# Mean square for the normalisation by two float32r products with a matrix of ones

## The chip, the cores and the metric

The kernel runs on one core of a Trainium2 chip. The metric is the device time of one execution in microseconds (us); the median over several runs is compared. All times below are in us unless ns is written. The engines are called as in the profile: PE is TensorE, PEld its loading of weights, DVE is VectorE, ACT is ScalarE, POOL is GpSimd, SP is SyncE.

## The reference

Attention with two kinds of masks is followed by a gated feed-forward layer with a normalisation by the root of the mean square (RMS) ahead of it. Everything is float32.

```python
# attention: batch 8, heads 8, 576 positions, 64 per head; a window of 32 (first heads)
# or of 32 steps of 4 (last heads)
attn = softmax(mask(q @ k.T / 8)); attn_out = attn @ v
x = attn_out.transpose(0, 2, 1, 3).reshape(4608, 512)
# feed-forward: 512 -> 1536 -> 512
rms = np.sqrt(np.mean(x * x, axis=-1, keepdims=True) + 1e-06)
xn = x / rms * rms_g
g = xn @ w_gate
val = xn @ w_val
return (g * (1.0 / (1.0 + np.exp(-g))) * val) @ w_out
```

## The kernel before

The 4608 tokens are cut into 16 units of 288 (U). x is held transposed: 128 of the 512 features on the partitions, tokens along the row, so a unit's x is four tiles of 128 x 288 (`xraw`). While the feed-forward products of one unit run on TensorE, the attention of the next is slipped in between. The first unit's products are plain float32; from the second unit on each float32 operand is split into a high part rounded to float32r and the remainder, also in float32r, and a product is three float32r products (`three`, lines 632 to 634).

**The plan.** Nothing is scheduled by the compiler: the program's order is written by hand. A unit's feed-forward is 36 steps (`now`): for each of 12 slices j of the hidden layer one step for the gate (g), one for the value (v) and one for the projection (acc) of the slice before. A dictionary `events` says in which step an attention piece has its scores (q, line 499, tile s), its transposition (t), its product with v (o), and in which step the unit's sum of squares (`rms_sum`) and its broadcast (`rms_apply`) stand. These TensorE instructions come at the end of the step, behind its twelve large products. Work on other engines is put off with `later(dt, rank, fn)`: it is issued dt steps on, at the step's start, in order of rank. EARLY and LAST set the steps of a unit's first and last scores, SCORES those of the second and third unit.

**The normalisation.** ScalarE squares each tile of x (line 433), VectorE or GpSimd adds the four up (line 439), which leaves 128 x 288 squares (`sq`). `rms_sum` sums over the partitions: three float32 products per unit, with 96 tokens of the squares as weights and a column `inv` of 1/512 as the moving operand, two columns wide, so that the mean of each token lands on a partition (96 x 3, tile rps). `rms_root`, one step later, adds 1e-6 on VectorE (line 546), takes the power -0.5 on GpSimd (line 547) and splits the result (rst_hi, rst_lo, lines 552 and 553). One step later `spread` multiplies the identity with each part, the high part on VectorE (line 561), the low one on ScalarE (line 565): tiles rd, 96 x 288 with the values on diagonals. `rms_apply` multiplies a matrix of ones with both (line 581, tile bps): every partition then has every token's factor, and VectorE applies it to x (line 595).

**Neighbours on the engines.** Around this stand, on VectorE, the gate's and value's products (lines 676 and 689, tile th), the masked maximum of scores (lines 366 and 371), the low part of q (line 349, tile qs) and the softmax's sum and reciprocal (lines 390 and 391); on GpSimd the low parts of the hidden layer (line 701, hlo), of k (line 340, ks) and the softmax's scaling (line 397).

## Time and profile before

| what | value |
|---|---|
| median of 3 runs | 1138.24 us (1136.36 to 1138.36) |
| the profiled execution's span, first to last instruction | 1137.1 us |
| what the median has beyond that span | 1.1 us |
| TensorE busy | 1119.5 us, 98% of the span |
| VectorE, ScalarE, GpSimd busy | 70%, 62%, 54% |
| the sums of squares (line 539): instructions, busy on TensorE | 96 in 16 units, 9.5 us |
| the broadcasts (line 581): instructions, busy on TensorE | 32, 7.4 us |
| mean granted TensorE clock | 0.997 |

One execution was profiled; its rows are read against its own span. A row of the view in order of time has start, length, engine, line, operation, tiles (written <- read), shape and, in brackets, how long the engine had been idle and what ended that. Records of TensorE overlap, since its products are pipelined: the distance from start to start is what one costs. A row of the view by groups has a count behind the x, then busy time, mean length of one in ns, and the idle time before them.

### The profile page before, as it was taken

What the parts mean: (1) busy time and instruction counts of PE and PEld (TensorE: products, weight loads), DVE (VectorE), ACT (ScalarE), POOL (GpSimd) and SP (SyncE); (2) the same over time, 40 slices, a digit from 0 to 9 for tenths busy, and PEclk for the clock granted to TensorE, in tenths of its full rate; (3) what the DMA queues carried; (4) which work ended last, traced back from release to release, by engine and by line L of the source; (5) the groups of instructions that cost most, each with busy time, mean ns of one, the idle gap of its engine ahead of it and who ended that gap; (6) DMA issues with size and microseconds to landing.
All of it is one profiled execution on the core that took longest, in us unless ns stands there. A gap on an engine that the chain in (4) does not pass through costs nothing.

```text
span 1137.1 us, 25931 instructions
## 1 busy us (share of the span) xinstructions
PE 1119.5 (98%) x8371; PEld 1088.7 (96%) x8371; DVE 795.5 (70%) x2875; ACT 708.7 (62%) x2608; POOL 615.7 (54%) x1071
## 2 busy tenths in 40 slices
PE   9999889999999999999999999999999999999998
PEld 7787779999999999999999999999999999999998
DVE  6889878858667585876758677675867768586411
ACT  6795665657667566675757666575766757576311
POOL 8223677656556455565646556564655646465311
PEclk9999989999999999999999999999999999999999
DMA  9665221212213031221213122121311212120000
GB/s 246 181 228 198 78 59 40 82 40 71 64 34 98 27 95 42 79 62 31 81 40 103 41 63 74 36 84 39 86 51 54 87 34 79 42 80 15 6 17 22
DMA packets 61545, 82.19 MB, mean 72 GB/s; under 512 B 7298, under 2 KB 41090, under 8 KB 61410
## 3 DMA queue, kind: packets, MB, share of 16 engines
q1 hardware_dynamic: 61410, 80.54, 23.7%
q8 instruction: 67, 1.10, 0.4%
q14 instruction: 68, 0.56, 0.2%
HBM read 71.08 MB, written 9.44 MB: 71 GB/s over the span
## 4 chain that ended last, share of the span: by engine, by line
PE 91%; DVE 5%; ACT 1%; issue 1%; DMA 1%; POOL 1%; POOLq 0%; SPq 0%; ACTq 0%
PE acc L632 9%; PE v L632 8%; PE g L632 8%; PE acc L633 8%; PE acc L634 8%; PE v L633 8%; PE g L633 8%; PE v L634 8%; PE g L634 8%; PE s L499 3%; PE o L487 3%; PE acc L629 2%; PE v L629 1%; PE o L488 1%; PE busy L749 1%; PE g L629 1%
## 5 line engine op out<-in xcount | busy, mean ns | idle before, releaser
L701 POOL TENSOR_TENSOR hlo<-th,hhi 128x288 fp32r<-128x288 f32 x180 | 146.3, 813 | 200.9 <-ACT hhi L700 150.6
L634 PE MATMUL acc<-hhi,lo 128*128 128x288 f32 x720 | 212.6, 295 | 0.0
L397 POOL TENSOR_SCALAR t<-t,sum 72x72 f32<-72x72 f32 (+3 forms) x414 | 153.1, 382 | 69.7 <-DVE sum L391 61.1
L634 PE MATMUL v<-xhi,lo 128*128 128x288 f32 x612 | 180.5, 295 | 0.0
L634 PE MATMUL g<-xhi,lo 128*128 128x288 f32 x612 | 180.3, 295 | 0.0
L700 ACT CAST hhi<-th 128x288 fp32r<-128x288 f32 x180 | 78.1, 434 | 155.7 <-DVE th L689 153.4
L381 ACT ACTIVATE t<-t,sum 96x128 f32<-96x128 f32 (+3 forms) x448 | 166.1, 375 | 11.4 <-DVE sum L371 10.9
L310 POOL TENSOR_TENSOR vlo<-vt,vhi 128x128 fp32r<-128x128 f32 x196 | 94.1, 480 | 107.6 <-ACT vhi L306 92.7
L671 ACT ACTIVATE th<-g 128x288 f32<-128x288 f32 x180 | 73.8, 410 | 106.1 <-PE g L634 86.3
L634 PEld LDWEIGHTS acc<-hhi,lo 128*128 128x128 f32 x720 | 135.9, 189 | 0.0
L427 DVE TENSOR_TENSOR xraw<-o,xraw 64x72 f32<-64x72 f32 (+1 forms) x364 | 99.1, 272 | 50.6 <-ACT xraw L417 44.5
L676 DVE SCALAR_TENSOR_TENSOR th<-th,g 128x288 f32<-128x288 f32 x180 | 80.4, 447 | 68.3 <-ACT th L671 68.3
L634 PEld LDWEIGHTS v<-xhi,lo 128*128 128x128 f32 x612 | 115.4, 189 | 0.0
L634 PEld LDWEIGHTS g<-xhi,lo 128*128 128x128 f32 x612 | 115.2, 188 | 0.0
L632 PE MATMUL g<-xhi,hi_g 128*128 128x288 f32 x357 | 111.0, 311 | 0.1
L632 PE MATMUL acc<-hhi,hi_o 128*128 128x288 f32 x360 | 111.0, 308 | 0.0
L366 DVE TENSOR_TENSOR t<-s,mask 96x256 f32<-96x256 f32 (+3 forms) x196 | 71.5, 365 | 53.5 <-PE s L499 42.6
L689 DVE TENSOR_TENSOR th<-th,v 128x288 f32<-128x288 f32 x180 | 81.4, 452 | 38.0 <-PE v L634 30.1
L633 PE MATMUL acc<-hlo,hi_o 128*128 128x288 f32 x360 | 107.3, 298 | 0.0
L340 POOL TENSOR_TENSOR ks<-qk,ks 128x288 fp32r<-128x288 f32 (+2 forms) x110 | 104.5, 964 | 0.3 <-ACT ks L335 0.3
L417 ACT COPY xraw<-o 64x72 f32<-64x72 f32 (+1 forms) x364 | 94.1, 259 | 11.7 <-PE o L488 9.6
L633 PE MATMUL g<-xlo,hi_g 128*128 128x288 f32 x322 | 94.9, 295 | 0.0
(192 smaller groups left out, 3597.0 us busy)
## 6 DMA issues: line engine op xcount, KB each, us to landing
qk<-in_qk_dram SPq DMA_DIRECT2D x60, 288.0 KB, 2.8
vt<-in_v_dram SPq DMA_DIRECT2D x196, 64.0 KB, 1.9
qk<-in_qk_dram SPq DMA_DIRECT2D x30, 352.0 KB, 3.0
out_dram<-ot SPq DMA_DIRECT2D x64, 144.0 KB, 1.9
qk<-in_qk_dram SPq DMA_DIRECT2D x30, 304.0 KB, 2.8
raw<-in_w_gate_dram SPq DMA_DIRECT2D x12, 512.0 KB, 4.6
raw<-in_w_val_dram SPq DMA_DIRECT2D x12, 512.0 KB, 4.9
raw<-in_w_out_dram SPq DMA_DIRECT2D x12, 512.0 KB, 4.2
```

Source lines behind the costliest of these rows:

```text
L310: G.tensor_tensor(out=vl, in0=vs.pop(b), in1=vh, op=ALU.subtract)
L340: ek.tensor_tensor(out=ks[:, 1, :nkt], in0=kr, in1=ks[:, 0, :nkt], op=ALU.subtract)
L381: A.activation(out=t[:nq, a, :n], in_=t[:nq, a, :n], func=AF.Exp, scale=-1.0, bias=sm[:nq, a, 0:1], accum_out=sm[:nq, a, 1:2] if u or i % ...
L397: (V if u == 0 and (c, i) > (NC - 1, 0) else G).tensor_scalar(out=t[:nq, a, :n], in0=t[:nq, a, :n], scalar1=sm[:nq, a, 3:4], scalar2=1.0, ...
L417: A.copy(out=to[a * D:(a + 1) * D], in_=o[a * D:(a + 1) * D, (2 + a) * nq:(3 + a) * nq])
L427: V.tensor_tensor(out=to[rows], in0=o[rows, a * nq:(a + 1) * nq], in1=to[rows], op=ALU.add)
L632: PE.matmul(out, wh[:, cc, :], xh, start=start, stop=False)
L633: PE.matmul(out, wh[:, cc, :], xl, start=False, stop=False)
L634: PE.matmul(out, wl[:, cc, :], xh, start=False, stop=stop)
L676: V.scalar_tensor_tensor(out=t, in0=t, scalar=1.0, in1=g, op0=ALU.add, op1=ALU.mult)
L689: V.tensor_tensor(out=t, in0=t, in1=v_ps[:, :U], op=ALU.mult)
L701: G.tensor_tensor(out=lo, in0=t, in1=hi, op=ALU.subtract)
```

## The change

From the second unit on, the sum over the partitions is taken by two float32r products in place of three float32 ones. The added-up squares are split into a high and a low float32r part (ScalarE casts, VectorE subtracts). Both are moving operands of 288 columns, and the weights are 96 columns of ones. Every one of the 96 partitions then holds all 288 sums. The wanted value of token q of block i on partition q is picked out on VectorE: a product with the identity (96 x 288), a sum along each block of 96, and the factor 1/512 with the 1e-6 added. The power, the splitting and the broadcast are as before. The plan moves too: EARLY and LAST are one less, so that the attention of each unit from the fourth on comes one step sooner; the sum stays 28 steps behind the unit's start and the broadcast 30 (from the third unit on), and in the second unit the sum comes one step later.

```diff
-EARLY, LAST = -9, 17
+EARLY, LAST = -10, 16
...
             later(1, 0.4, lambda: (V if c == NC - 1 or u == 1 else G).tensor_tensor(out=xsq[u], in0=xsq[u], in1=sq, op=ALU.add))
+            if u and c == NC - 1:
+                later(1, 0.45, lambda: square_parts(u))
...
+    def square_parts(u):
+        hi = sb.tile([P, U], F32R, tag="tmp", name=f"sqhi_{u}", bufs=2)
+        A.copy(out=hi, in_=xsq[u])
+        lo = sb.tile([P, U], F32R, tag="tmp", name=f"sqlo_{u}", bufs=2)
+        V.tensor_tensor(out=lo, in0=xsq[u], in1=hi, op=ALU.subtract)
+        xsq[u] = hi, lo
+
     def rms_sum(u):
-        r_ps = ps.tile([QB, NB, 2], F32, tag="o", name=f"rps_{u}")
-        for i in range(NB):
-            PE.matmul(r_ps[:, i, :], xsq[u][:, i * QB:(i + 1) * QB], inv, start=True, stop=True)
-        later(1, 0.1, lambda: rms_root(u, r_ps))
         if u == 0:
+            r_ps = ps.tile([QB, NB, 2], F32, tag="o", name=f"rps_{u}")
+            for i in range(NB):
+                PE.matmul(r_ps[:, i, :], xsq[u][:, i * QB:(i + 1) * QB], inv, start=True, stop=True)
+            later(1, 0.1, lambda: rms_root(u, r_ps))
             later(1, 6, spread_first)
+            return
+        r_ps = ps.tile([QB, U], F32, tag="o", name=f"rps_{u}")
+        for k, part in enumerate(xsq.pop(u)):
+            PE.matmul(r_ps, ones[:, :QB], part, start=k == 0, stop=k == 1)
+        later(1, 0.1, lambda: rms_root(u, r_ps.rearrange("p (i q) -> p i q", i=NB)))
 
     def rms_root(u, r_ps):
         r = sb.tile([QB, NB], F32, tag="rst", name=f"rst_{u}", bufs=2)
-        V.tensor_scalar(out=r, in0=r_ps[:, :, 0], scalar1=1e-6, scalar2=None, op0=ALU.add)
-        G.tensor_tensor(out=r, in0=r, in1=mhalf, op=ALU.pow)
         if u == 0:
+            V.tensor_scalar(out=r, in0=r_ps[:, :, 0], scalar1=1e-6, scalar2=None, op0=ALU.add)
+            G.tensor_tensor(out=r, in0=r, in1=mhalf, op=ALU.pow)
             rst[u] = [r]
             return
+        d = sb.tile([QB, NB, QB], F32, tag="tmp", name=f"diag_{u}", bufs=2)
+        V.tensor_tensor(out=d, in0=r_ps, in1=ident[:QB, None, :QB].to_broadcast([QB, NB, QB]), op=ALU.mult)
+        V.tensor_reduce(out=r, in_=d, axis=mybir.AxisListType.X, op=ALU.add)
+        V.tensor_scalar(out=r, in0=r, scalar1=1.0 / DM, scalar2=1e-6, op0=ALU.mult, op1=ALU.add)
+        G.tensor_tensor(out=r, in0=r, in1=mhalf, op=ALU.pow)
...
-        events.setdefault(last + (4 if u == 1 else 3), {})["sum"] = u
-        events.setdefault(last + (4, 7, 5)[min(u, 2)], {})["apply"] = u
+        events.setdefault(last + (3, 5, 4)[min(u, 2)], {})["sum"] = u
+        events.setdefault(last + (4, 7, 6)[min(u, 2)], {})["apply"] = u
```

What that makes of the order on the engines is shown for one unit in the middle of the program; numbers behind names are buffers, and line numbers of the changed kernel are its own. On VectorE, from the root to the spreading of its high part, before (th is the hidden layer's product with v, t and s are scores, qs the low part of q, rd the diagonals that bps is made of):

```order
L689 TENSOR_TENSOR th_9_7807<-th_9_7807,v_9_7817 128x288
L546 TENSOR_SCALAR rst_7835<-rps_7830 96x3
L561 TENSOR_TENSOR rd_0_7868<-ident,rst_hi_7838 96x288
L366 TENSOR_TENSOR t_0_1_7874<-s_0_1_7865,mask 96x256
L371 ISA t_0_1_7874,sum_89<-s_0_1_7865,t_0_1_7874 96x128
L349 TENSOR_TENSOR qs_2_7850<-qk_2_7446,qs_2_7850 64x288
```

And in the changed kernel:

```order
L708 TENSOR_TENSOR th_9_7849<-th_9_7849,v_9_7859 128x288
L566 TENSOR_TENSOR diag_7880<-rps_7875,ident 96x288
L567 TENSOR_REDUCE rst_7879<-diag_7880 96x3
L568 TENSOR_SCALAR rst_7879<-rst_7879 96x3
L366 TENSOR_TENSOR t_0_1_7893<-s_0_1_7872,mask 96x256
L371 ISA t_0_1_7893,sum_89<-s_0_1_7872,t_0_1_7893 96x128
L349 TENSOR_TENSOR qs_2_7856<-qk_2_7460,qs_2_7856 64x288
L390 TENSOR_REDUCE sum_88<-sum_88 96x2
L391 RECIPROCAL sum_88<-sum_88 96x2
L580 TENSOR_TENSOR rd_0_7919<-ident,rst_hi_7885 96x288
```

The root is three instructions in place of one, and rd now stands behind the maximum of a piece of scores, the low part of q and the softmax's small instructions, which followed it before.

On GpSimd around the power, before:

```order
L701 TENSOR_TENSOR hlo_8_7766<-th_8_7745,hhi_8_7765 128x288
L310 TENSOR_TENSOR vlo_1321<-vt_0_1_7635,vhi_1320 128x128
L547 TENSOR_TENSOR rst_7835<-rst_7835,mhalf 96x3
L552 CAST rst_hi_7838<-rst_7835 96x3
L553 TENSOR_TENSOR rst_lo_7839<-rst_7835,rst_hi_7838 96x3
L701 TENSOR_TENSOR hlo_9_7843<-th_9_7807,hhi_9_7842 128x288
L340 TENSOR_TENSOR ks_2_7815<-qk_2_7446,ks_2_7815 128x288
L340 TENSOR_TENSOR ks_3_7848<-qk_3_7480,ks_3_7848 128x288
```

And in the changed kernel:

```order
L720 TENSOR_TENSOR hlo_8_7805<-th_8_7779,hhi_8_7804 128x288
L340 TENSOR_TENSOR ks_2_7834<-qk_2_7460,ks_2_7834 128x288
L569 TENSOR_TENSOR rst_7879<-rst_7879,mhalf 96x3
L571 CAST rst_hi_7885<-rst_7879 96x3
L572 TENSOR_TENSOR rst_lo_7886<-rst_7879,rst_hi_7885 96x3
L720 TENSOR_TENSOR hlo_9_7890<-th_9_7849,hhi_9_7889 128x288
L340 TENSOR_TENSOR ks_3_7854<-qk_3_7499,ks_3_7854 128x288
```

One low part of k (ks) moved ahead of the power; hlo still follows the root's low part.

On TensorE around the sum, the tail of the step, before:

```order
L634 MATMUL v_9_7817<-xhi_3_6931,lo_2001 128x288
L539 MATMUL rps_7830<-inv,sq_0_7146 96x2 x3
L632 MATMUL acc_0_7153<-hhi_8_7765,hi_o_2068 128x288
L633 MATMUL acc_0_7153<-hlo_8_7766,hi_o_2068 128x288
L634 MATMUL acc_0_7153<-hhi_8_7765,lo_2069 128x288
```

And in the changed kernel:

```order
L653 MATMUL v_9_7859<-xhi_3_6978,lo_2007 128x288
L501 MATMUL s_0_1_7872<-ks_0_7394,qs_0_7428 96x256
L501 MATMUL s_0_1_7872<-ks_1_7426,qs_1_7462 96x256
L555 MATMUL rps_7875<-sqhi_7826,ones 96x288
L555 MATMUL rps_7875<-sqlo_7828,ones 96x288
L651 MATMUL acc_0_7209<-hhi_8_7804,hi_o_2074 128x288
```

Two products stand in place of three, and the scores that followed the next step (acc) now stand ahead of the sum. From here to bps there are still two steps, acc and g, with one pair of scores behind g.

## The prediction, made before the change was run

> **What bounds the kernel now.** I read the page first, then the order of time on each engine around one sum of squares.
>
> ```profile
> span 1137.1 us, 25931 instructions
> PE 1119.5 (98%) x8371; PEld 1088.7 (96%) x8371; DVE 795.5 (70%) x2875; ACT 708.7 (62%) x2608; POOL 615.7 (54%) x1071
> PE 91%; DVE 5%; ACT 1%; issue 1%; DMA 1%; POOL 1%; POOLq 0%; SPq 0%; ACTq 0%
> ```
>
> TensorE is the bound: 98% busy, 91% of the chain of waits. What is taken off its queue is won in full, and a wait put into it is lost in full, unless another wait of TensorE shrinks. So the question has two halves: what the float32r sum saves on TensorE, and whether the longer way from the sum to the broadcast (bps) still fits between the two. TensorE in order of time, in the unit whose sum starts at 458.14 (columns: start, length, engine, line, operation, tiles, shape):
>
> ```profile
> 458.00 0.30 PE L634 MATMUL v<-spare,lo 128*128 128x288 f32 x1
> 458.14 0.59 PE L539 MATMUL rps<-inv,sq 128*96 128x2 f32 x6
> 458.81 0.30 PE L633 MATMUL acc<-hlo,hi_o 128*128 128x288 f32 x1
> ...
> 460.26 0.40 PE L499 MATMUL s<-ks,qs 128*96 128x256 f32 x2
> 460.50 0.29 PE L632 MATMUL g<-xhi,hi_o 128*128 128x288 f32 x1
> ...
> 462.08 0.43 PE L581 MATMUL bps<-rd,ones 96*128 96x288 f32 x2
> 462.36 0.30 PE L632 MATMUL v<-xhi,hi_o 128*128 128x288 f32 x1
> ```
>
> A product of 288 columns takes 0.132 of the queue from start to start (g's twelve from 460.50 to 462.08, 1.58). From L634 at 458.00 to L633 at 458.81 there are 0.81; without the sum it would be two steps, 0.265. The six passes of rps cost 0.545.
>
> **What is saved.** Two float32r products of 288 columns replace them. The nearest row is bps itself, two such products in 0.28 (462.08 to 462.36); I take 0.265. That is 0.28 less in each of 15 units, 4.2 in all, on the bounding engine. Bounds: 0.25 to 0.30 per unit.
>
> **What is added, and the slack it has.** I count in a normal unit (13 of them, the third to the fifteenth) from the start of rps, t = 0. VectorE, GpSimd and ScalarE before:
>
> ```profile
> 458.34 0.46 DVE L689 TENSOR_TENSOR th<-th,v 128x288 f32<-128x288 f32 x1 [0.25 <-PE v L634]
> 458.77 0.16 DVE L546 TENSOR_SCALAR rst<-rps 96x3 f32<-96x3 f32 x1
> 460.15 0.45 DVE L561 TENSOR_TENSOR rd<-ident,rst_hi 96x288 fp32r<-96x288 f32 x1 [1.23 <-POOL rst_hi L552]
> 460.70 0.42 DVE L366 TENSOR_TENSOR t<-s,mask 96x256 f32<-96x256 f32 x1
> ...
> 461.69 1.73 DVE L349 TENSOR_TENSOR qs<-qk,qs 64x288 fp32r<-64x288 f32 x1
> 463.64 0.17 DVE L391 RECIPROCAL sum<-sum 96x2 f32<-96x2 f32 x1
> 463.72 0.49 DVE L595 SCALAR_TENSOR_TENSOR xraw<-xraw,gs,bps 128x288 f32<-128x288 f32 x1
> ```
>
> ```profile
> 459.00 0.86 POOL L547 TENSOR_TENSOR rst<-rst,mhalf 96x3 f32<-96x3 f32 x1 [3.63 <-DVE rst L546]
> 459.94 0.18 POOL L552 CAST rst_hi<-rst 96x3 fp32r<-96x3 f32 x1
> 460.20 0.46 POOL L553 TENSOR_TENSOR rst_lo<-rst,rst_hi 96x3 fp32r<-96x3 f32 x1
> 460.62 0.80 POOL L701 TENSOR_TENSOR hlo<-th,hhi 128x288 fp32r<-128x288 f32 x1
> ```
>
> ```profile
> 460.69 0.91 ACT L565 ACTIVATE rd<-ident,rst_lo 96x96 fp32r<-96x96 f32 x3
> ```
>
> Before, VectorE does the root's scalar at 0.63 to 0.79, GpSimd's power ends at 1.72, VectorE's rd runs from 2.01 to 2.46, ScalarE's rd ends at 3.46, and bps stands at 3.94. The slack is 0.48. In the changed kernel bps would come, with no wait, at 0.265 for the sums, 1.58 for acc and 1.58 for g (460.50 to 462.08) and 0.24 for the scores that now stand behind g (460.26 to 460.50): 3.67.
>
> Step by step, now. The sums end at 0.13 + 0.29 = 0.42, and th's product (0.46 long, its v group ends 0.24 earlier because a pair of scores comes between) ends there too. The product with the identity has rd's shape: 0.46. For the reduction of 288 elements, and for two shapes that follow, these rows stand (the last two give least, median and longest in ns):
>
> ```profile
> L389 DVE TENSOR_REDUCE sum<-t 96x2 f32<-96x256 f32 x2 | 0.8, 414 | 0.8 <-ACT t L381 0.8
> L349 DVE TENSOR_TENSOR qs<-qk,qs x112: 454/456/1726, 107.7 to 1024.7; 64x288 fp32r<-64x288 f32 x112
> L553 POOL TENSOR_TENSOR rst_lo<-rst,rst_hi x15: 193/462/464, 104.5 to 1064.5; 96x3 fp32r<-96x3 f32 x15
> ```
>
> 256 elements cost 0.41; 288 cost 0.47 if all of it goes with the elements and 0.41 if none does; I take 0.45. With gaps of 0.04 between dependent instructions and 0.16 for the scalar, VectorE is through at 0.46 + 0.46 + 0.04 + 0.45 + 0.04 + 0.15 = 1.60; it was 0.79. GpSimd (gaps of 0.08, from 458.93 to 459.00 and from 459.86 to 459.94) has the power done at 2.54 and rst_hi at 2.80, and rst_lo could start at 2.88.
>
> The order matters more than these 0.8. rd is issued one step of the plan after the root, and what the same step puts ahead of it now stands on VectorE between them: the mask and maximum of the scores that moved one step up (L366 and L371, 0.99 from 460.70 to 461.69), qs's low part (0.46 alone) and L390, L391. So VectorE starts qs at 1.60 + 0.03 + 0.99 = 2.62 and ends it at 3.08; rd comes 0.30 later (from 463.42, the end of qs, to 463.72), at 3.38. GpSimd's rst_lo meets qs as it met rd before (0.46 long beside it, 0.19 alone) and ends 0.04 behind it, at 3.12; hlo then runs from 3.08 to 3.88. So rd, with two inputs in SBUF, arrives in the middle of a GpSimd instruction with two inputs in SBUF. What this does:
>
> ```profile
> 566.65 1.00 DVE L349 TENSOR_TENSOR qs<-qk,qs 64x288 fp32r<-64x288 f32 x1
> ```
>
> ```profile
> 566.52 0.81 POOL L701 TENSOR_TENSOR hlo<-th,hhi 128x288 fp32r<-128x288 f32 x1 [0.83 <-ACT hhi L700]
> 567.28 1.10 POOL L340 TENSOR_TENSOR ks<-qk,ks 128x320 fp32r<-128x320 f32 x1
> ```
>
> VectorE's 0.46 became 1.00: it ended 0.32 after hlo did (567.33). So rd ends at 3.88 + 0.32 = 4.20. In the Trainium skill, "SBUF — State Buffer", section "Who interferes with whom", a VectorE instruction with two SBUF inputs and a GpSimd instruction that reads SBUF exclude each other for a whole instruction; the rows above agree, and by that rule the identity product, with one input in PSUM, and the reduction go free. The lag from rd to bps:
>
> ```profile
> 38.27 0.46 DVE L571 TENSOR_TENSOR rd<-ident,rst 96x288 f32<-96x288 f32 x1 [0.76 <-POOL rst L547]
> ```
>
> ```profile
> 38.87 0.72 PE L581 MATMUL bps<-rd,ones 96*128 96x288 f32 x2 [0.16 <-DVE rd L571]
> ```
>
> 0.14 from 38.73 to 38.87. bps starts at 4.34 in place of 3.67: a wait of 0.67. ScalarE's part (rst_lo 3.12, + 0.04 + 0.91 = 4.07) is ready for the second product. Net in a normal unit: 0.67 - 0.28 = +0.39; 13 units: **+5.1**.
>
> The splitting of the squares is a cast on ScalarE and a subtraction on VectorE:
>
> ```profile
> 455.64 0.46 DVE L439 TENSOR_TENSOR sq<-sq,sq 128x288 f32<-128x288 f32 x1 [0.51 <-ACT sq L433]
> L700 ACT CAST hhi<-th 128x288 fp32r<-128x288 f32 x180 | 78.1, 434 | 155.7 <-DVE th L689 153.4
> ```
>
> The squares were added up 2.0 before rps (456.10); LAST and EARLY bring that a step, about 1.8, ahead. Cast, subtraction and gaps take about 1.0 of those 3.8, under products of g and v on TensorE: nothing is paid. Uncovered it would be 1.0 per unit.
>
> **The first and the last changed unit.** The last one has no scores of a successor:
>
> ```profile
> 1062.61 0.45 DVE L689 TENSOR_TENSOR th<-th,v 128x288 f32<-128x288 f32 x1 [0.62 <-PE v L634]
> ```
>
> ```profile
> 1062.41 0.59 PE L539 MATMUL rps<-inv,sq 128*96 128x2 f32 x6
> ```
>
> There th's product ends 0.65 after rps begins (1063.06 less 1062.41), so the chain is 0.2 later: root 1.80, power 2.74, rst_hi 2.99, rd 3.03 to 3.49, rst_lo 3.54, ScalarE 3.58 to 4.49; the second product, due at 0.265 + 1.58 + 1.58 + 0.13 = 3.56, starts at 4.63. A wait of 1.07, net +0.8. The second unit lies where VectorE decodes weights:
>
> ```profile
> 104.70 1.45 DVE L561 TENSOR_TENSOR rd<-ident,rst_hi 96x288 fp32r<-96x288 f32 x1
> 104.70 1.13 POOL L167 TENSOR_SCALAR raw<-raw 128x1024 f32<-128x1024 f32 x1
> 100.00:112.00 12.00, 12.00 (x56) 9.44 (x54) 11.88 (x18) 6.23 (x13) 4.27 (x6) 1.00 0.35 119
> ```
>
> (The last row is from the view by windows: the stretch, then busy time of PE, its loads, VectorE, ScalarE, GpSimd.)
> VectorE is busy 11.88 of 12.00 there, so 0.46 + 0.46 + 0.45 more work stays as delay. In that unit the sum also moves one group closer to bps. With rd after the decoding pieces that stand ahead of it, and 0.14 to TensorE, bps comes some 0.6 late by the same steps (an estimate, bounds 0 and 1.5; net +0.35), and of the 1.4 of delay I take 0.5 as reaching TensorE (bounds 0 and 1.4).
>
> **Sum.** 5.1 + 0.8 + 0.35 + 0.5 = +6.7 on the span of 1137.1, that is 1143.8. The median of the runs, 1138.24, lies 1.1 above that span, and a span of 1143.8 answers to **1145**.
>
> **The rivals.** (a) *No collision*: rd falls into a gap of GpSimd and ends at 3.84. The second product then waits for ScalarE's part, 4.07 + 0.14 against 3.80: 0.41, net +0.13; 13 x 0.13 + 1.65 = +3.3, 1141.5. For it: at least half of L349's 112 went free (the median is 456 ns); against: hlo follows rst_lo at once in the rows above. (b) *The chain fits*, the one on the other side: if the identity product and the reduction are much cheaper than the rows nearest to them, rd passes ahead of hlo, bps waits for nothing and only the saving is left: -4.2, 1134. It decides from 0.67 less on VectorE, that is 0.24 for the two in place of 0.91. For it: TensorE was never late here before; against it: a product of this shape has never taken under 0.45, and ScalarE's part at 4.07 misses as well. (c) *qs too is held*: if VectorE arrives 0.25 later, rst_lo is in flight and hlo follows; in the row at 461.69 qs took 1.73, through two GpSimd instructions. qs then ends at 4.18, rd at about 5.2: net +1.4, 13 x 1.4 + 1.65 = +20, 1158. (d) *VectorE's backlog reaches the next group*: after bps it has low parts, normalising, scores and th's product before g may overwrite v's bank. With the prices above (0.46 to 1.0 for the low part, 0.49, 0.99, 0.46 twice, 0.3 for the small ones and some 0.35 for the part of the transposed scores) it is through near 8.1; TensorE, late by 0.67, wants the bank near 8.2. That is too close to call covered. Were it 0.35 late in each unit: +4.6 more, 1149.5.
>
> **How the numbers follow.** Forecast 0.43, (a) 0.19, (b) 0.13, (c) 0.08, (d) 0.17. The range 1136.5 to 1152 takes in the forecast, (a) and (d) with the bounds of the saving (0.03 per unit), of the reduction (0.04) and of the decoding stage (1.4 once); (b) and (c) stay out. A change below 0.2% (2.3 us) can't be told from none here. Faster is (b), 0.13; the same is the near side of (a), 0.15; slower the rest, 0.72.
>
> **What would show it.** rps as two products in some 0.27; L567 near 0.45; VectorE through with the root at 1.6; rd beginning near 3.4 and 0.8 long beside hlo; idle time of about 0.67 before bps in 13 units, released by VectorE, and about 1.1 in the last, released by ScalarE. It is wrong if bps has no idle time before it (then the saving stands alone), or if the wait is above 1.2 (then qs is held too).

## The result, and the profile after

The changed kernel takes **1205.78 us** (1204.58 to 1211.72, 4 runs) where the kernel before took 1137.82 beside it (1136.36 to 1138.36, 4 runs): a ratio of 1.061, 95% interval 1.059 to 1.064, so 68 us slower. The prediction had slower, 1145; the direction is right, and the change is ten times as large as forecast. The page after, with the lines that answer to those shown of before. It is of the run that took 1211.72, 6 above the median, whose granted clock is the lowest of the four (0.982, the others 0.986 to 0.990); the account below is made with it:

```profile
span 1209.9 us, 25908 instructions
...
PE 1146.6 (95%) x8311; PEld 1102.2 (91%) x8311; DVE 826.3 (68%) x2920; ACT 711.7 (59%) x2623; POOL 623.0 (51%) x1071
...
PE 73%; DVE 16%; ACT 5%; issue 3%; POOL 2%; DMA 0%; POOLq 0%; ACTq 0%; DVEq 0%
```

TensorE is no longer busy throughout, and VectorE's share of the chain went from 5% to 16%. What TensorE waits for (columns: tile and line, the releaser, us in total, times, longest):

```profile
PE o L489 <- DVE xraw L427: 19.2, 13, 1.5
PE bps L600 <- DVE rd L580: 10.4, 14, 1.9
PE g L652 <- DVE xlo L632: 9.1, 13, 1.4
PE g L651 <- DVE pt L456: 4.0, 12, 0.6
...
PE bps L600 <- ACT rd L584: 1.1, 2, 0.5
```

Before, the waits for xlo, for o's VectorE part and for rd (but 0.2 in the first unit) weren't there. The wait for bps, which I had predicted, is the second of them. The other three are at another place: at the boundary of two units, where the next unit's first groups begin. A wait costs more than its idle time. Idle time is counted from the end of the record ahead of it, while the next product normally starts 0.16 before that end (scores of 0.40 at 460.26, g at 460.50). The distances between the first products of successive steps count all of it. Worked out from the traces, mean of the fifth to the fifteenth unit (step 35 to the fourteenth), before and the difference of the others to it (step 30 holds the broadcast, step 28 the sum, which stands in 27 in "room at end"; step 0 is the next unit's first group; the four columns on the right are the experiments e1, e4, e16 and e17 below):

```
step            before  changed  plan    end     first   room
                                 alone   only    piece   at end
28                2.04   +0.02   +0.21   -0.18   -0.00   -0.46
29                1.89   -0.30   -0.22   -0.08   +0.00   -0.08
30                1.85   +1.11   +0.21   +0.75   -0.00   +0.00
31 to 33          5.37   +0.14   -0.01   +0.40   -0.06   -0.03
34, 35            3.96   -0.13   -0.13   +0.01   -0.09   -0.07
0                 1.70   +3.44   +3.45   +0.00   -0.00   +0.00
1                 2.29   +0.38   +0.43   -0.05   -0.12   +0.00
2                 1.70   +0.74   +0.46   +0.00   -0.00   -0.00
the whole unit   67.03   +5.43   +4.44   +0.92   -0.24   -0.35
```

Of 5.4 per unit, 4.6 arise in the steps 0 to 2 and about 0.8 in the steps 28 to 30.

**The way from the sum to bps** came in its steps almost as predicted. One normal unit, whose sums start at 481.93, VectorE, GpSimd and TensorE in order of time:

```profile
482.39 0.45 DVE L566 TENSOR_TENSOR diag<-rps,ident 96x288 f32<-96x288 f32 x1
482.88 0.45 DVE L567 TENSOR_REDUCE rst<-diag 96x3 f32<-96x288 f32 x1
483.36 0.17 DVE L568 TENSOR_SCALAR rst<-rst 96x3 f32<-96x3 f32 x1
...
485.18 1.09 DVE L580 TENSOR_TENSOR rd<-ident,rst_hi 96x288 fp32r<-96x288 f32 x1
```

```profile
483.60 0.86 POOL L569 TENSOR_TENSOR rst<-rst,mhalf 96x3 f32<-96x3 f32 x1 [2.81 <-DVE rst L568]
484.53 0.39 POOL L571 CAST rst_hi<-rst 96x3 fp32r<-96x3 f32 x1
...
485.16 0.80 POOL L720 TENSOR_TENSOR hlo<-th,hhi 128x288 fp32r<-128x288 f32 x1
```

```profile
481.93 0.29 PE L555 MATMUL rps<-sqhi,ones 128*96 128x288 f32 x1
...
486.42 0.50 PE L600 MATMUL bps<-rd,ones 96*128 96x288 f32 x2 [0.66 <-DVE rd L580]
```

The root is done 1.60 after the sums begin (483.53 less 481.93), rd meets hlo and lasts 1.09. bps starts 4.49 after the sums, where 3.67 would be without a wait: it is 0.82 late, 0.66 of it idle.

**The boundary**, 10 us later, is what I had not looked at. VectorE, ScalarE, GpSimd and TensorE:

```profile
496.46 2.29 DVE L632 TENSOR_TENSOR xlo<-xraw,xhi 128x288 fp32r<-128x288 f32 x1 [1.32 <-ACT xhi L631]
...
499.66 0.46 DVE L349 TENSOR_TENSOR qs<-qk,qs 64x288 fp32r<-64x288 f32 x1
500.14 0.52 DVE L427 TENSOR_TENSOR xraw<-o,xraw 64x96 f32<-64x96 f32 x2
```

```profile
495.51 0.47 ACT L417 COPY xraw<-o 64x96 f32<-64x96 f32 x2
495.99 0.43 ACT L631 CAST xhi<-xraw 128x288 fp32r<-128x288 f32 x1
```

```profile
495.57 1.07 POOL L340 TENSOR_TENSOR ks<-qk,ks 128x416 fp32r<-128x416 f32 x1
496.61 0.79 POOL L720 TENSOR_TENSOR hlo<-th,hhi 128x288 fp32r<-128x288 f32 x1
497.38 1.06 POOL L340 TENSOR_TENSOR ks<-qk,ks 128x416 fp32r<-128x416 f32 x1
```

```profile
498.80 0.40 PE L652 MATMUL g<-xlo,hi_g 128*128 128x288 f32 x1 [0.94 <-DVE xlo L632]
...
500.81 0.66 PE L489 MATMUL o<-pt,vhi 128*128 128x384 f32 x1 [1.48 <-DVE xraw L427]
```

The last low part of x (L632) takes 0.44 where nothing holds it (the shortest of this instruction before). It arrives in the middle of a row of three GpSimd instructions with two inputs in SBUF and ends 0.31 after the last of them. g waits 0.94 for it. Behind it on VectorE stand a piece's maximum, a low part of q, and then the addition of the first attention output (L427), which must have read o's bank before the second output may be written: o waits 1.48. Before the change the same instruction met one GpSimd instruction and took 0.89:

```profile
538.76 0.89 DVE L613 TENSOR_TENSOR xlo<-xraw,xhi 128x288 fp32r<-128x288 f32 x1 [0.31 <-ACT xhi L612]
```

Then the **clock** goes. Stretches of one or two times 3.41 us; after each start and end, busy time of PE, its loads, VectorE, ScalarE and GpSimd, then the granted clock:

```profile
497.20:500.60 3.40, 1.19 (x7) 0.72 (x6) 3.29 (x9) 1.26 (x6) 1.86 (x3) 1.00 0.00 0
500.70:504.10 3.40, 3.29 (x14) 3.32 (x15) 2.99 (x13) 0.77 (x3) 1.40 (x3) 0.50 0.70 181
```

After 3.4 us in which TensorE worked 1.19, the next 3.4 run at half the clock. Mean granted clock was 0.997 and is 0.982 in this run: thirteen windows of 3.41 at half the clock, where there were two. At half a window each, 11 x 1.71 = 18.8 more are lost to it, at most (TensorE also stood idle in a part of them), and less in the other three runs.

The 72.8 between the spans are thus, in idle time: 32.3 at the boundary (19.2 + 9.1 + 4.0), 11.5 before bps, 18.8 of clock, less 4.2 saved; some 14 are left. An estimate from the rows above: 54 waits at the 0.16 that idle time leaves out are 9 of them. First products after a wait are also slower (bps's two here stand 0.21 apart, not 0.13), and the second unit has other waits.

### The profile page after: what moved, and what is told of

Read it like the earlier page. It is cut to its first block, busy times and chain, and to the rows that moved or that the text cites. A ratio compares the mean times of both kernels' runs of the same rounds, so it can differ in the third digit from the quotient of the medians.

```text
span 1209.9 us, 25908 instructions
## 1 busy us (share of the span) xinstructions
PE 1146.6 (95%) x8311; PEld 1102.2 (91%) x8311; DVE 826.3 (68%) x2920; ACT 711.7 (59%) x2623; POOL 623.0 (51%) x1071
## 4 chain that ended last, share of the span: by engine, by line
PE 73%; DVE 16%; ACT 5%; issue 3%; POOL 2%; DMA 0%; POOLq 0%; ACTq 0%; DVEq 0%
PE v L651 7%; PE v L652 7%; PE g L651 7%; PE v L653 7%; PE g L652 6%; PE g L653 6%; PE acc L651 6%; PE acc L652 6%; PE acc L653 6%; PE s L501 2%; DVE xlo L632 2%; PE o L489 2%; DVE qs L349 2%; DVE t L371 2%; PE v L648 2%
## 5 line engine op out<-in xcount | busy, mean ns | idle before, releaser
L720 POOL TENSOR_TENSOR hlo<-th,hhi 128x288 fp32r<-128x288 f32 x180 | 150.1, 834 | 178.7 <-ACT hhi L719 147.8
L653 PE MATMUL v<-xhi,lo 128*128 128x288 f32 x612 | 184.2, 301 | 0.0
L310 POOL TENSOR_TENSOR vlo<-vt,vhi 128x128 fp32r<-128x128 f32 x196 | 97.6, 498 | 118.1 <-ACT vhi L306 103.5
L427 DVE TENSOR_TENSOR xraw<-o,xraw 64x72 f32<-64x72 f32 (+1 forms) x364 | 99.1, 272 | 43.2 <-ACT xraw L417 39.4
L653 PEld LDWEIGHTS v<-xhi,lo 128*128 128x128 f32 x612 | 119.0, 194 | 0.0
L454 ACT CAST pt<-v 104x144 fp32r<-104x144 f32 (+3 forms) x65 | 19.1, 294 | 137.4 <-DVE th L708 137.4
```

Source lines behind the costliest of these rows:

```text
L310: G.tensor_tensor(out=vl, in0=vs.pop(b), in1=vh, op=ALU.subtract)
L427: V.tensor_tensor(out=to[rows], in0=o[rows, a * nq:(a + 1) * nq], in1=to[rows], op=ALU.add)
L653: PE.matmul(out, wl[:, cc, :], xh, start=False, stop=stop)
L720: G.tensor_tensor(out=lo, in0=t, in1=hi, op=ALU.subtract)
```

## The experiments

All ratios are to the kernel before, run beside them, with 95% intervals. The runs are called e1 to e18, as their labels begin.

**Which half of the change costs?** Plan alone, and sum alone.

Plan alone (e1) is the kernel before with

```diff
-EARLY, LAST = -9, 17
+EARLY, LAST = -10, 16
...
-        events.setdefault(last + (4 if u == 1 else 3), {})["sum"] = u
-        events.setdefault(last + (4, 7, 5)[min(u, 2)], {})["apply"] = u
+        events.setdefault(last + (3, 4, 4)[min(u, 2)], {})["sum"] = u
+        events.setdefault(last + (4, 7, 6)[min(u, 2)], {})["apply"] = u
```

and sum alone (e2) the changed kernel with

```diff
-EARLY, LAST = -10, 16
+EARLY, LAST = -9, 17
...
-        events.setdefault(last + (3, 5, 4)[min(u, 2)], {})["sum"] = u
-        events.setdefault(last + (4, 7, 6)[min(u, 2)], {})["apply"] = u
+        events.setdefault(last + (3, 5, 3)[min(u, 2)], {})["sum"] = u
+        events.setdefault(last + (4, 7, 5)[min(u, 2)], {})["apply"] = u
```

> The kernel before with EARLY and LAST one less and the sum and the broadcast kept 28 and 30 steps behind the unit's start: the plan of the changed kernel with the old float32 sum. Theory P (the shift of the attention by one step is what costs: it puts the copies of the first attention output and two low parts of k ahead of or beside the low part of x that the next unit's first group needs): nearly all of the +68 stays, less the 10.4 of waits before bps and plus the 4.2 that the sum costs more: 1190 to 1205, with waits before the next unit's first groups (xlo, o) as in the changed kernel. Theory V (VectorE's longer way from the sum to bps, 0.81 more at the root and a late bps, is what pushes the next unit's first groups back): 1136 to 1142, no such waits. Both needed: 1145 to 1180.

e1 measured 1193.91, ratio 1.049 (1.047 to 1.051). The waits of o and of g for xlo are to the digit those of the changed kernel:

```profile
PE o L487 <- DVE xraw L427: 19.2, 13, 1.5
PE g L633 <- DVE xlo L613: 9.1, 13, 1.4
```

So the move of the attention by one step alone, with the old sum, costs 56 of the 68, low clock included (0.982 here too), and the theory that VectorE's longer way is behind it falls. The sum and its way add 12 on top.

> The changed kernel with EARLY and LAST back at -9 and 17 and the sum and the broadcast 28 and 30 steps behind the unit's start: the float32r sum on the old plan. Theory P: near the old time, with the wait before bps that the longer way costs (0.4 to 0.7 in 13 units less the 0.28 saved): 1137 to 1148, and hardly any wait before the next unit's first groups. Theory V: most of the loss stays, 1185 to 1206. Both needed: 1145 to 1180.

e2 measured 1164.38, 1.024 (1.022 to 1.025): above theory P and far below V. The number lies where "both needed" had it, but for another reason: the boundary is quiet, and the sum itself is dearer than I had said. Waits of TensorE, and one of VectorE:

```profile
PE bps L600 <- DVE rd L580: 8.9, 14, 1.9
PE bps L600 <- ACT rd L584: 8.0, 15, 0.5
```

```profile
DVE sqlo L542 <- ACT sqhi L540: 17.4, 15, 1.3
```

The split of the squares stands at the head of VectorE's queue and waits 1.2 for ScalarE's cast; the scores' maximum and th's products behind it are late, the root is through 2.63 after the sums begin instead of 1.60, and bps waits for both parts. The step that the plan was moved by does give the split its room (7.5 of that wait in the changed kernel), but pays for it at the other end.

> The changed kernel without the product with the identity and the reduction; the root takes one column of each block of the sums (this part of the computation is left out, so the factors are wrong). That takes 0.94 off VectorE's way to bps. Theory P: only the wait before bps goes (10.4 in all, and some of the low clock behind it), the waits before the next unit's first groups stay: 1188 to 1199. Theory V: those waits go as well, 1132 to 1145.

```diff
-        d = sb.tile([QB, NB, QB], F32, tag="tmp", name=f"diag_{u}", bufs=2)
-        V.tensor_tensor(out=d, in0=r_ps, in1=ident[:QB, None, :QB].to_broadcast([QB, NB, QB]), op=ALU.mult)
-        V.tensor_reduce(out=r, in_=d, axis=mybir.AxisListType.X, op=ALU.add)
-        V.tensor_scalar(out=r, in0=r, scalar1=1.0 / DM, scalar2=1e-6, op0=ALU.mult, op1=ALU.add)
+        V.tensor_scalar(out=r, in0=r_ps[:, :, 0], scalar1=1.0 / DM, scalar2=1e-6, op0=ALU.mult, op1=ALU.add)
```

e3 measured 1196.63, 1.052 (1.050 to 1.053). The wait before bps is gone but for the second unit (0.9 and 0.5), and 19.2 and 9.2 stay at the boundary. VectorE's 0.9 more has nothing to do with them.

**Which end of the move?** The plan spreads the fourteen pieces between EARLY and LAST in whole steps. From -9 to 16 (e4, the changed kernel) they stand at -9, -7 and so on to 15, as before, and only the last moves, to 16. From -10 to 17 (e16, the kernel before) only the first moves. The whole change put all of them on -10, -8 and so on to 16.

```diff
-EARLY, LAST = -10, 16
+EARLY, LAST = -9, 16
```

```diff
-EARLY, LAST = -9, 17
+EARLY, LAST = -10, 17
```

> The changed kernel with EARLY alone back at -9: of each unit's fourteen attention pieces only the last now comes a step sooner, the first ones stand where they stood before, so the next unit's first attention output falls in step 35 again and not in step 34. Theory B (the shift costs at the boundary of two units, where the first output's copies and the low parts of k stand beside the low part of x that the next unit's first group needs): the 19 and 9 of waits there and the low clock behind them go, the wait before bps stays: 1142 to 1155. Theory E (the shift costs at its other end, where the last pieces come closer to the sum): most of the loss stays, 1180 to 1206.

e4 ("end only") measured 1153.10, 1.013 (1.012 to 1.015): theory B. The split still has its room and the boundary costs nothing (the column "end only"). What is left of its waits, but for the second unit, is the second product of bps:

```profile
PE bps L600 <- ACT rd L584: 7.1, 15, 0.5
```

The table has 0.75 for it per unit in step 30, and 0.40 more in the steps 31 to 33, in delays too short to be counted as waits.

> The kernel before with EARLY alone at -10: of each unit's fourteen pieces only the first comes a step sooner (its output in step 34), the other thirteen stand where they stood. Theory 1 (the first output's copy and addition beside the last low part of x are enough): 1175 to 1195. Theory R (it takes the row: GpSimd's low parts of k come with the fourth piece, and the second output two steps behind the first needs its bank): 1136 to 1150, with line 613 at most 0.9 long and no wait of o.

e16 ("first piece") measured 1133.57, 0.9966 (0.9955 to 0.9977): theory R by its signs (line 613 at most 0.90, no wait of o), and 2 below its range, a small gain. So neither end of the row costs by itself. That points to the pieces between: with all fourteen on even steps the move costs 56, with the first alone nothing. VectorE was held less than before in this run: its low parts of x (tile xlo) took 11.3 in all where they had taken 17.0, and this is its group of qs, before and then here (count, busy time, mean ns):

```profile
L349 DVE TENSOR_TENSOR qs<-qk,qs 64x288 fp32r<-64x288 f32 x112 | 85.1, 760 | 9.3 <-ACT qs L344 6.3
```

```profile
L349 DVE TENSOR_TENSOR qs<-qk,qs 64x288 fp32r<-64x288 f32 x112 | 70.8, 632 | 8.1 <-ACT qs L344 5.0
```

**Which wait at the boundary is the cause?** Each was taken away by another order, in the changed kernel: GpSimd's low parts of k one step later (e5, e8, e9), the last split of x sooner in its step (e6, e8, e9), the addition of the first output sooner in its step (e9, e10).

```diff
-                split(*nxt, (1, 2, 2, 3), G, V)
+                split(*nxt, (1, 3, 2, 3), G, V)
-                split(nxt[0], nxt[1] + 1, (2, 3, 3, 4), G, V)
+                split(nxt[0], nxt[1] + 1, (2, 4, 3, 4), G, V)
...
-                later((2, 3, 4, 5)[c], 0.6, lambda c=c: part(c))
+                later((2, 3, 4, 5)[c], 0.6 if c < 3 else 0.45, lambda c=c: part(c))
...
-                later(1, 4, lambda: add(*o, o_ps))
+                later(1, 0.55 if o[1] + o[2] == 0 else 4, lambda: add(*o, o_ps))
```

> The changed kernel with GpSimd's low parts of k (line 340) one step later, as they stood at the boundary before, and the last split of x (its cast on ScalarE and its low part on VectorE) ahead of the hidden layer's cast and the first output's copy. Theory G (the low part of x starves behind a row of GpSimd instructions: 2.29 in place of 0.45): it takes at most 1.2 and is done 1.5 to 2 sooner, so g waits no more and o waits 0.5 to 1.0 in place of 1.5; with the low clock behind these waits 1165 to 1190. Theory C (only the late cast counts): as in the run beside this one that moves the cast alone. Neither: above 1200.

e5 as it ran moved only the low parts of k; what its expectation says of the split of x is in e8. It measured 1198.49, 1.053 (1.052 to 1.055), between the outcomes that had been set down for the two moves together. VectorE's groups of xlo and of qs in the changed kernel, then here:

```profile
L349 DVE TENSOR_TENSOR qs<-qk,qs 64x288 fp32r<-64x288 f32 x112 | 65.6, 586 | 3.5
...
L632 DVE TENSOR_TENSOR xlo<-xraw,xhi 128x288 fp32r<-128x288 f32 x16 | 21.7, 1357 | 14.0 <-ACT xhi L631 14.0
L632 DVE TENSOR_TENSOR xlo<-xraw,spare 128x288 fp32r<-128x288 f32 x7 | 11.1, 1582 | 7.8 <-ACT spare L631 7.8
```

```profile
L349 DVE TENSOR_TENSOR qs<-qk,qs 64x288 fp32r<-64x288 f32 x112 | 88.5, 790 | 3.5
...
L632 DVE TENSOR_TENSOR xlo<-xraw,xhi 128x288 fp32r<-128x288 f32 x16 | 8.4, 524 | 14.0 <-ACT xhi L631 14.0
L632 DVE TENSOR_TENSOR xlo<-xraw,spare 128x288 fp32r<-128x288 f32 x7 | 3.3, 468 | 7.8 <-ACT spare L631 7.8
```

xlo is 21.1 shorter (32.8 to 11.7), qs 22.9 longer. The starving is cured where it was seen and stands on another instruction. g no longer waits for xlo, but 18.3 for pt in place of 4.0, and o 12.8. The clock stays at 1.00.

> The changed kernel with the last split of x alone sooner, GpSimd's order as it is. Theory G: VectorE's low part arrives some 0.8 sooner, in the middle of the first low part of k, and still stands until GpSimd's row is through or gets in after the first one: between 1190 and 1206, and line 632's longest ones above 2. Theory C (the cast behind the first output's copy is what is late): line 632 at 0.45 to 0.9, 1165 to 1185.

e6 measured 1210.37, 1.064 (1.059 to 1.068): theory G by its sign, line 632 above 2. The time is 4 above its range; two of the four runs lie at 1205 and 1206 with a granted clock of 0.99, two at 1214 and 1216 with 0.98. Starting sooner, the low part stands longer and through the same three GpSimd instructions:

```profile
491.03 3.19 DVE L632 TENSOR_TENSOR xlo<-xraw,xhi 128x288 fp32r<-128x288 f32 x1 [0.42 <-ACT xhi L631]
```

```profile
491.03 1.08 POOL L340 TENSOR_TENSOR ks<-qk,ks 128x416 fp32r<-128x416 f32 x1
492.07 0.81 POOL L720 TENSOR_TENSOR hlo<-th,hhi 128x288 fp32r<-128x288 f32 x1
492.83 1.07 POOL L340 TENSOR_TENSOR ks<-qk,ks 128x416 fp32r<-128x416 f32 x1
```

> The changed kernel with both moves: GpSimd's low parts of k one step later and the last split of x ahead of the hidden layer's cast and the first output's copy. (The run e5_klow_later_x_sooner, against what its expectation says, moved only the low parts of k; this one is what was meant.) Theory G+C (the starved low part of x first, the late cast behind it): line 632 at 0.45 to 0.9 and 0.4 to 0.8 sooner than in e5, so the waits of o (12.8 there) and of g for pt (18.3 there) shrink by that in each unit: 1165 to 1185. If GpSimd's instructions that were moved only hold the next one of VectorE with two inputs in SBUF instead: within 5 of e5, 1194 to 1204.

e8 measured 1192.20, 1.048 (1.046 to 1.049): close to the second outcome, and 6 below e5. o waits 7.3 in place of 12.8, g for pt still 17.8.

> As e8_both_moves, and VectorE's addition of the first attention output's second half (line 427 for the first piece alone) ahead of the low part of x in place of behind the scores' maximum and the low part of q. Theory O (the bank of o, one buffer that the second output needs while VectorE still has not read the first, is what the moved attention runs into): the wait of o goes, 5 to 20 less than e8. If the addition only pushes the low part of x back: g waits for xlo again, within 5 of e8 or above.

e9 measured 1190.34, 1.046 (1.044 to 1.048). The wait of o is down to 1.8, but the total hardly moves, 2 where 5 to 20 had been expected: v now waits 6.9 for pt, g 17.1.

> The changed kernel with the addition of the first output's second half ahead of the low part of x alone. Theory O: the 19.2 of waits of o go, line 632 still starves (g waits 0.7 to 1.2 per unit); a window of TensorE is then never half idle, so the granted clock stays at 1.00 and its some 18 go as well: 1160 to 1182. If line 632's starving (theory G) is the larger part: above 1190.

e10 measured 1196.04, 1.051 (1.050 to 1.053): theory G's number, not O's. The 19.2 went, and v waits 10.2 for pt (2.6 in the changed kernel), s 7.8 (3.6). The granted clock, 0.993, did not stay at 1.00 either.

So no single wait is the cause. Each comes from VectorE being behind at that place, and freeing one instruction lets TensorE run into the next. All three moves together win back 15 of 68, about what the clock had cost: it is 0.998 to 1.000 in e9's runs.

**Parity?** A theory that holds at the boundary and falls by the time: that the heavy steps of the attention now meet the steps in which VectorE makes low parts of x.

In e12 (changed kernel) and e15 (kernel before) the move is by two steps, with sum and broadcast kept at 28 and 30; e13 is e12 with the sum at 27 from the fourth unit on; e14 is the changed kernel with the low parts of x exchanged between VectorE and GpSimd.

```diff
-EARLY, LAST = -10, 16
+EARLY, LAST = -11, 15
```

```diff
-            (V if c % 2 else G).tensor_tensor(out=lo, in0=x, in1=hi, op=ALU.subtract)
+            (G if c % 2 else V).tensor_tensor(out=lo, in0=x, in1=hi, op=ALU.subtract)
```

> The changed kernel with EARLY, LAST = -11, 15, one more step sooner, the sum and the broadcast kept at 28 and 30. Theory P: the waits at the boundary go, the waits before bps are those of e4_end_only (0.47 for ScalarE's part): 1144 to 1160. Theory S: 1205 to 1260.

> The kernel before with EARLY, LAST = -11, 15 and the float32 sum and the broadcast kept at 28 and 30: a move by two alone. Theory P: as before, 1135 to 1143. Theory S: above e1_plan_alone, 1195 to 1250.

> As e12_by_two, with the sum at 27 from the fourth unit on and the broadcast at 30, three steps between them. Theory P: no wait before bps and none at the boundary, so the saving of 0.28 per unit is left, less what the second unit loses (3): 1132 to 1142. Theory S: 1200 or more.

> The changed kernel with the low parts of x exchanged: the first and third tile's on VectorE, the second and fourth's on GpSimd. Theory P: VectorE's steps 33 and 35 lose 0.46 and more of starving, 32 and 34 gain them; the waits of g for xlo and of o shrink by half or more: 1150 to 1185. Theory S: the amount of work is the same, above 1195. The fourth's on GpSimd stands behind the hidden layer's low part there, 0.81 long, and may itself be late for g.

e12 measured 1203.51, 1.058 (1.056 to 1.060); e15, with the old sum, 1186.34, 1.043 (1.041 to 1.044); e13, with room, 1176.72, 1.034 (1.033 to 1.036); e14, the swap, 1183.46, 1.040 (1.039 to 1.042). By the time none of the four fits theory P but the swap, at the edge of its range, and e12 and e15 stay below theory S. At the boundary it fits: counted as in the table, the steps 0 to 2 lose nothing in e12, e13 and e15 (-0.07 to -0.08), and 1.4 in e14, where they lost 4.6 in the changed kernel. But a move by two costs nearly as much as by one at other places, in e12 and e15 1.8 in step 33 and 0.9 each in the steps 35 and 5. The waits of e12:

```profile
PE g L651 <- DVE pt L456: 20.1, 26, 0.9
PE o L489 <- DVE xraw L614: 19.8, 13, 1.6
```

The first attention output now comes while VectorE still reads bps, which has the same bank; the step's transposed scores share their bank with the next g. e13 has 2.8 left of the wait of o, since its bps comes without a wait, and the 20 for pt. The swap wins 22 back without curing: the waits of o go, but g waits 9.1 for GpSimd's low part in place of VectorE's.

**The sum's own cost.** Four runs start from e4. In e11 VectorE makes the low part of rd too:

```diff
-                if p is r_hi:
+                if True:
                     V.tensor_tensor(out=d, in0=ident[:QB, None, :QB].to_broadcast([QB, NB, QB]),
```

> As e4_end_only, with the low part of the diagonals made by VectorE (one product with the identity, 0.46) in place of ScalarE (three, 0.91). The second product of bps waited 0.47 for ScalarE there. If only that wait is in the way: 0.3 to 0.47 less in 15 units, 1145 to 1149. If VectorE's 0.46 more pushes what follows: 1152 to 1160.

e11 measured 1179.07, 1.037 (1.035 to 1.039), 26 worse than "end only" and outside both outcomes. The second rd, 0.46 when free, is held behind hlo and ks:

```profile
L580 DVE TENSOR_TENSOR rd<-ident,rst_lo 96x288 fp32r<-96x288 f32 x15 | 33.8, 2254 | 1.3
L580 DVE TENSOR_TENSOR rd<-ident,rst_hi 96x288 fp32r<-96x288 f32 x15 | 6.8, 454 | 18.2 <-POOL rst_hi L571 18.2
```

In e7 the eighth to the fourteenth piece come sooner, the last by two steps; the seventh and eighth (3 and 4) and the last two (14 and 15) then stand on successive steps, so that the sum has its room and stands at 27, three steps ahead of the broadcast:

```diff
-EARLY, LAST = -9, 16
+EARLY, LAST = -9, 15
...
-        events.setdefault(last + (3, 5, 4)[min(u, 2)], {})["sum"] = u
-        events.setdefault(last + (4, 7, 6)[min(u, 2)], {})["apply"] = u
+        events.setdefault(last + (3, 5, 5, 4)[min(u, 3)], {})["sum"] = u
+        events.setdefault(last + (4, 7, 7, 7)[min(u, 3)], {})["apply"] = u
```

> The changed kernel with EARLY -9 and LAST 15, the sum one step sooner (27 behind the unit's start, from the fourth unit on) and the broadcast where it was (30): three steps between them in place of two. If the way from the sum to bps and the boundary are all that costs, both are gone here and the saving of the sum is left: 1131 to 1142. If VectorE's 0.9 more per unit costs wherever it stands: 1143 to 1160. If the two last pairs of pieces, which now follow step on step, hold each other up: above 1150, with waits of s or o behind sum L371 or xraw.

e7 measured 1173.38, 1.031 (1.029 to 1.033): the third outcome by the time, though of the waits it named only that of o came. No wait before bps but in the second and the third unit; g waits 8.2 for th, 6.3 for pt, v 5.4 for pt and o 4.7. Counted as in the table, 1.5 of the 2.5 lost per unit lie in the steps 8 and 9, in which the pair of 3 and 4 is transposed. That pieces on successive steps are always too much for VectorE isn't shown: e4's last two stand on 15 and 16 and cost nothing of the kind. The first seven pieces stand as before, and the steps 0 to 2 lose nothing.

In e17 ("room at end") the pieces are those of e4, and only the sum comes sooner:

```diff
-        events.setdefault(last + (3, 5, 4)[min(u, 2)], {})["sum"] = u
+        events.setdefault(last + (3, 4, 4, 3)[min(u, 3)], {})["sum"] = u
```

> As e4_end_only (EARLY -9, LAST 16), with the sum one step sooner from the third unit's successor on (27 behind the unit's start), the broadcast at 30, and the second unit's sum back where it was. The split of the squares then stands in the step of the sum itself, and VectorE waits for ScalarE's half of it, as in e2_sum_alone. If the way from the sum to bps is the whole of e4's loss: no wait before bps, 1132 to 1141. If VectorE's idle time at the split and its 0.9 more push the boundary: 1145 to 1165.

e17 measured 1136.84, 0.9996 (0.9987 to 1.0006): the first outcome, no change against the kernel before, 69 less than the changed kernel. bps stands 5.27 after the sums, and from the fourth unit on it waits for nothing (in the third its second product waits 0.53 for ScalarE):

```profile
457.06 0.29 PE L555 MATMUL rps<-sqhi,ones 128*96 128x288 f32 x1
...
462.33 0.44 PE L600 MATMUL bps<-rd,ones 96*128 96x288 f32 x2
```

In the fifth to the fifteenth unit it gains 0.35 per unit, 0.28 of which is the saving that the change was to bring; the second unit gives part of it back (from the first unit's bps to its own there are 70.26, it was 68.89).

And e18 adds e16's first piece to it:

```diff
         q_at = [LAST - (LAST - EARLY) * (nb - 1 - k) // (nb - 1) for k in range(nb)]
+        q_at[0] -= 1
```

> As e17_room_at_end, with the first piece of each unit from the fourth on one step sooner (at -10; the second stays at -7). e16_first_piece gained 0.24 per unit in the fifth to the fifteenth, e17_room_at_end 0.35, and lost 1.4 once in the second unit. If they add up: 12 times 0.6 less 1.4, about 5.5 below the kernel before, 1130 to 1134. If the first piece's copy and the earlier sum meet on VectorE: 1136 or more.

e18 measured 1137.93, 1.000 (0.999 to 1.001): they don't add up. Its unit takes 66.78, where 66.44 would have been the sum of both gains and e17 alone has 66.68. The first piece's gain of 0.33 in step 35 is there, and so is its loss of 0.24 in step 34. New is that step 31 loses 0.35, where e16 lost 0.15 and e17 nothing.

## Why the prediction was wrong, point by point

- **What bounds the kernel** (TensorE, so that a wait put into its queue is lost in full): right, and stronger than I used it, since lost waits also cost clock.
- **Saved, 0.28 per unit**: right. The sums stand 0.26 from the first to acc (481.93 to 482.19), six passes took 0.545.
- **The chain in a normal unit**: right in its steps, too small in its price. Identity product 0.45 (0.46 said), reduction 0.45 (0.45), root at 1.60 (1.60), power at 2.53 (2.54), rd beginning at 3.25 (3.38), held by hlo and done at 4.34 (4.20), bps at 4.49 (4.34). That the idle time before bps is 0.66 where I said 0.67 is luck: my 0.67 was the lateness against 3.67, and that is 0.82; idle time leaves out 0.16 of it. Over the 13 units the idle time is (10.4 - 1.9) / 13 = 0.65. So the cost was undersized: in the table the steps 28 to 30 lose 0.83; plan alone loses 0.20 there, which leaves 0.63 for the sum against the 0.39 of my net. The 0.15 by which bps comes later than I said and the 0.08 by which its two products stand further apart are that difference.
- **The last unit**: the wait for ScalarE is there; the second product starts 4.43 after the sums (1138.74 less 1134.31) where 4.63 was said and 3.56 was due, so it is 0.87 late where 1.07 was said. **The second unit**: 1.9 and 0.5 before bps where 0.6 stood with a bound of 1.5: the bound was too narrow.
- **"LAST and EARLY bring that a step, about 1.8, ahead ... nothing is paid"**: this is the step that failed. I took the move of the plan as the cover for the split and looked at what it frees. It is a change of its own: it moves fourteen pieces, each with instructions on four engines, in thirteen units. Plan alone, it costs 56. The trace of before showed the place: xlo 0.89 long beside a GpSimd instruction, in the row quoted above, and I had followed the unit only up to bps and, in rival (d), to the bank of the next group.
- **"Uncovered it would be 1.0 per unit"**: near. "Sum alone", without the cover, lost 27, and "end only", which has it, 16; the 11 between them are 0.75 per unit. But those 16, which the sum costs with its cover and a quiet boundary, are more than twice the +6.7 of my whole forecast: the second unit lost 3.2 (72.04 from the first unit's bps to its own, 68.89 before) where 0.85 was forecast, the second product of bps waited for ScalarE as in rival (a), but 0.62 late in place of 0.41, and the 0.40 per unit in the steps 31 to 33 behind it had no term.
- **Rival (d)**, VectorE's backlog reaching the next group, had the right engine and nearly the place, at 4.6 for 0.35 per unit. In fact the waits at the boundary are 32 and the clock up to 19; the backlog came from the move, not from a late bps (without the identity product and the reduction it stays). In the changed kernel (a), (b) and (c) did not occur.
- **What would show it wrong**: I had named two signs, both at bps. bps passed both, and the forecast was off by 60. Signs should have been named for every place that the change moves.

What stays open: which pieces set the boundary off. The first alone (e16) and the eighth to the last (e7) don't, which points to the second to the seventh, alone or with others; no run moved these by themselves. It was shown that the move by itself costs 56, that GpSimd's row holds VectorE, and that the waits replace one another; a single wait that is the cause was not found.

## What to carry to other kernels

A plan's offset that is changed to make room is an edit with a price of its own: run it alone first, and count what it moves at both ends. Where an engine that takes its instructions in the order of the program is busy without a gap ahead of the bound, a wait that is cured there comes back at its next instruction; look for a move that leaves that stretch as it is (here: the last piece alone, and one step more for the long way) rather than for the next cure. And signs that would show a forecast wrong belong at every place that the edit touches, not only where it was reckoned.

## What the runs showed of the hardware

**Half idle is enough to lose the clock.** I had expected nothing of the clock. In the traces it falls to half for 3.41 us (or twice that), and always on one grid of such windows in a run. In the changed kernel, after the first 200 us, all nine falls followed a window with TensorE busy 0.29 to 0.50 of it (records joined), and windows with 0.58 and more kept the clock, but for three that followed a window already at half (0.77 to 0.81). In e1 0.17 to 0.51 lost it and 0.56 did not; in e6 0.53 kept it and 0.55 lost it. In e10 0.55 lost it, and 0.48, close to the end of the run, kept it. So the edge lies near a half in these runs, and by the busy share alone not sharper than 0.48 to 0.55. Two waits of 0.94 and 1.48 that fall into one window cost up to 1.7 more, the half of a window. The Trainium skill, "TensorE: Matmul & The Clock Gate", Part 1, section "What's actually happening", gives the same window, 3413 ns and running freely, and lets the clock fall after an idle window; here no window was idle. A window with less idle time is followed by full clock:

```profile
572.30:575.70 3.40, 2.27 (x16) 2.12 (x17) 3.16 (x13) 1.71 (x8) 1.38 (x3) 1.00 0.46 114
575.80:579.20 3.40, 3.40 (x28) 3.33 (x26) 2.87 (x13) 1.91 (x9) 1.52 (x3) 1.00 0.28 97
```

**VectorE doesn't get its turn at the next GpSimd instruction.** With two inputs in SBUF it stood through two or three GpSimd instructions in a row (2.29 and 3.19 in place of 0.45, rows above), though in other places it got in after one (rd, 1.09). "SBUF — State Buffer", section "Who interferes with whom", in the Trainium skill says that the one blocks the other for a whole instruction, and that the order of issue decides who blocks. Who comes next among those that stand it does not say, and that is what decided here between 0.9 and 3.2: at 496.46 VectorE's record had begun before that of hlo at 496.61, and hlo still went first.
